# Regrouping the last weight tiles' rows of y: one late group of 16 rows for all batches and a third mid group moved on the SP queue

## The chip, the cores and the metric

The kernel runs on one NeuronCore of a Trainium2 chip. The metric is the device time of one execution in microseconds, as the median of five runs. The engines named below are PE (matmul; PEld is its weight load), DVE, ACT, POOL and SP. SP does no arithmetic here: it only issues DMAs. DMAs issued by SP, ACT and POOL each have a queue.

## What is computed

Attention with a forget gate on 8 batches, 8 heads, 576 positions and head size 64 gives x (8 x 576 x 512). Then x is mixed in the frequency domain: the first 64 modes of a real FFT over the positions are each multiplied by their own complex 512 x 512 matrix, and the inverse FFT gives y.

```
X = np.fft.rfft(x, axis=1)
Xr, Xi = (np.real(X[:, :n_modes]), np.imag(X[:, :n_modes]))
Yr = np.einsum('bmd,mde->bme', Xr, w_r) - np.einsum('bmd,mde->bme', Xi, w_i)
Yi = np.einsum('bmd,mde->bme', Xr, w_i) + np.einsum('bmd,mde->bme', Xi, w_r)
Y[:, :n_modes] = Yr + 1j * Yi
y = np.fft.irfft(Y, n=S, axis=1)
u = x + y
return (u + np.maximum(u @ w_ch, 0.0))
```

The inverse FFT is a matmul with a constant basis: per batch, 128 rows (64 modes, real and imaginary) by 576 positions. The kernel also needs u @ w_ch; it forms it as x @ w_ch plus the basis times (Y @ w_ch), so that each group of rows of Y is needed twice: as it is (called t=0) and times w_ch (t=1).

## The kernel before

**Weights.** `moe_w_r` and `moe_w_i` (together 134 MB in float32) are streamed through a ring of bfloat16 tiles, one tile after the other, by DMAs that POOL issues (`emit_w_load`, `pool_dma` at L90). There are NT = 64 tiles. The first 32 run beside the attention and cover the first two quarters of the input channels for all modes. The last 32 cover the second half of the channels, two modes each; a tile's index g (0 to 31) names its modes, and so the four rows of Y per batch that it completes. `tile_of` (L84) gives the order: g = 16 to 31 first (tiles 32 to 47), then g = 0 to 15 (tiles 48 to 63). Every one of these tiles ends with `add_y` (L146), which writes its completed rows of Y, transposed (channels on the partitions), into `YTe` for g of 16 and more, else into one half of `YT2`.

**Three kinds of rows.** The 64 rows per batch of g = 16 to 31 are "early": `emit_y` turns them into rows for the inverse FFT, and `emit_part` (L843) adds their share to x and to x @ w_ch while the remaining weights still stream. The other 64 rows per batch come in two halves of 32:

- g = 0 to 7 (tiles 48 to 55) are the "mid" rows. `emit_mid(q)` (L834) is called twice, after tiles 56 and 57, each time for four batches: `y_rows` does four transposes (L773, t=0) and four matmuls with w_ch (L777, t=1), and DVE and ACT copy each batch's 32 rows straight to their place in the tile `yy`.
- g = 8 to 15 (tiles 56 to 63) are the "late" rows, ready only when the last tile is done. Batches 0 to 3 go through `y_rows` at L995 right after that tile, batches 4 to 7 at L1032, in the output loop, after job 3.

A compute engine can copy batch 0's late rows directly to their place in `yy` (L996, L1000). The other batches' rows must change partitions: they are copied to a tile `yl` (L997, L1001; L1039, L1041) and then moved by small DMAs on POOL's queue (`emit_moves`, L904), 32 rows x 1 KB each: six for batches 1 to 3, and later eight for batches 4 to 7.

**The output loop.** There are 20 output jobs, five for each pair of batches: four of 256 positions of one batch, and as the fifth (jobs 4, 9, 14, 19) the last 64 positions of both batches. For each job PE sums two results in PSUM: pu (t=0, that is u) and pz (t=1, that is u @ w_ch). Each is the stored partial sum, passed through an identity, plus the basis times `yy`'s mid and late rows, 64 rows in one matmul. PE's matmuls of both kinds appear at L786. ACT copies pu to `uo` (L952, `emit_u`), DVE forms relu(pz) + u (L959, `emit_o`), and SP issues the output DMA (L971, or two DMAs of 64 rows at L966 for a fifth job; in job 19 alone the second of them is on ACT's queue). pu and pz of even and odd jobs have two PSUM places, so the sum pz of job n+2 can start only when DVE has read that of job n. The second late group borrows the unused halves of job 4's places. ACT's copy of job n+1 is written ahead of DVE's step of job n.

Of the kernel before, what the change touches and what calls it, by code (L numbers as in the profile page):

```python
# [9 lines left out]
BF16 = mybir.dt.bfloat16  # L10
# [11 lines left out]
def kernel(  # L22
# [11 lines left out]
    nc = tc.nc  # L34
    B, H, S, Dh = q.shape
    NM = moe_w_r.shape[0]
    D = H * Dh
# [5 lines left out]
    NDC = D // 128  # L43
# [22 lines left out]
    late = {}  # L66
# [17 lines left out]
    def tile_of(n):  # L84
        if n < NTH:
            return divmod(n, NG)
        return 2, (n - NTH + GL) % NTH

    def pool_dma(dst, src):
        tc.keep_in_program_order(nc.gpsimd.dma_start(dst, src))  # L90
# [36 lines left out]
    def emit_modes(n, fill=None):  # L127
# [17 lines left out]
            ]  # L145
        def add_y(mi0, mi1):  # L146
            n8 = (mi1 - mi0) * 2
            w = HM if g >= GL else HM // 2
            yt = late["YTe"] if g >= GL else late["YTs"][2 * g // GL]
            c0 = (g * nm + mi0) * 2 % w  # L150
            nc.vector.tensor_tensor(  # L151
                _strided(
                    yt[:, 0, 0, c0 : c0 + 1], [[B * w, NDC], [w, B], [1, n8]]
                ),
                _strided(A[:, 0, mi0, 0:1], [[nm * 2 * B, NDC], [1, B], [B, n8]]),
                _strided(
                    Yacc[:, 0, g * nm + mi0, 0:1],
                    [[NM * 2 * B, NDC], [1, B], [B, n8]],
                ),
                ALU.add,  # L160
            )
# [571 lines left out]
    with ExitStack() as bctx:  # L733
        bsb = bctx.enter_context(tc.tile_pool(name="bsb", bufs=1))
        YTe = bsb.tile([128, NDC, B, HM], BF16, name="YTe")
        YT2 = xtpool.tile([128, 2, NDC, B, HM // 2], BF16, tag="XT3", name="YT2")
        late["YTe"], late["YTs"] = YTe, [YT2[:, 0], YT2[:, 1]]
        HS = [slice(0, HM), slice(HM, 128)]
        BIe = [bsb.tile([128, SP], BF16, name=f"BIe{h}") for h in range(2)]
        BIl = bsb.tile([128, SP], BF16, name="BIl")  # L740
# [20 lines left out]

        yy = yls = xTs = None

        def row_slot(q, j, t, i):
            p0 = HM * ((j + t) % 2) + H2 * i
            return yy[p0 : p0 + H2, 1, 2 * q + j // 2, t, :]

        H2 = HM // 2

        def y_rows(yt, b0, ply, plw):  # L770
            cols = lambda eb: _strided(yt[:, eb, b0, 0:1], [[1, 128]])
            for eb in range(NDC):
                nc.tensor.transpose(  # L773
                    ply[:, eb * 128 : (eb + 1) * 128], cols(eb), ident_bf[:, :]
                )
            for eb in range(NDC):
                nc.tensor.matmul(  # L777
                    plw,
                    lhsT=cols(eb),
                    rhs=wch[:, eb, :],  # L780
                    start=(eb == 0),
                    stop=(eb == NDC - 1),
                )

        def add(p, lhsT, rhs, first):
            return nc.tensor.matmul(  # L786
# [7 lines left out]
        with ExitStack() as cctx:  # L794
# [39 lines left out]
            def emit_mid(q):  # L834
                pyw = psBig.tile([128, D], F32, tag="big", name="pyw")
                yp = psBig.tile([128, D], BF16, tag="big", name="yp")
                y_rows(YT2[:, 0], 4 * q, yp[:, :], pyw[:, :])
                for j in range(4):
                    rows = slice(H2 * j, H2 * j + H2)
                    nc.vector.tensor_copy(row_slot(q, j, 0, 0), yp[rows, :])  # L840
                    nc.scalar.copy(row_slot(q, j, 1, 0), pyw[rows, :])

            def emit_part(b, sb):  # L843
                pA = psBig.tile([128, D], F32, tag="big", name="pA")
# [19 lines left out]
            for bp in range(B // 2):  # L864
                parts += [(bp, None)]
                parts += [(b, sb) for b in (2 * bp, 2 * bp + 1) for sb in range(4)]
                parts += [(2 * bp, 4)]
            nx = done = 0
            while nmode < NT - 1:
                emit_modes(nmode)  # L870
                if nmode != late["nx"]:
                    next_w()
                nmode += 1
                if nmode == NTH + GL // 4:
                    open_late()
                if nmode > NTH + 6 and nmode % 4 and nx < B:
                    emit_xw(nx)
                    nx += 1
                if nmode > NT - GL:
                    assert nx == B  # L880
                    while done < (nmode - NT + GL) * (len(parts) - 2) // (GL - 2):
                        a, sb = parts[done]
                        emit_y(a) if sb is None else emit_part(a, sb)
                        done += 1
                if 0 <= nmode - NT + GL // 2 - 1 < 2:
                    emit_mid(nmode - NT + GL // 2 - 1)
            for a, sb in parts[done:]:
                emit_part(a, sb)

# [10 lines left out]
            for name in ("psE", "psU")  # L900
        )
        psPair = [{"u": psE, "z": psE}, {"u": psU}]

        def emit_moves(t, q, js):  # L904
            for j in js:
                pool_dma(
                    row_slot(q, j, t, 1), yls[q][H2 * j : H2 * j + H2, t, :]
                )

        def pieces(job):  # L910
            b, sb, nb = job
# [40 lines left out]
                nc.scalar.copy(uo[:, 0, bs, :], ps[0][:, bs, :])  # L952
            return uo

        def emit_o(job, ps, uo, split=False, last=False):
            b, sb, nb = job
            for i in range(2 if split else 1):
                bs = slice(i, i + 1) if split else slice(0, nb)
# [3 lines left out]
                )  # L962
                if sb == 4:
                    for h in range(2):
                        eng = nc.scalar if last and h else nc.sync
                        eng.dma_start(  # L966
                            out[b + h, 512:576, :],
                            uo[64 * h : 64 * h + 64, 1, 0, :],
                        )
                else:  # L970
                    nc.sync.dma_start(  # L971
                        out[b, 128 * sb : 128 * sb + 256, :].rearrange(
                            "(p r) e -> p r e", r=2
                        )[:, bs, :],
                        uo[:, 1, bs, :],
                    )
# [15 lines left out]
        ply = psL.tile([128, D], F32, tag="A", name="ply")  # L992
        ply = ply[:, 0 : D // 2].bitcast(BF16)
        plw = psL.tile([128, D], F32, tag="A", name="plw")
        y_rows(YT2[:, 1], 0, ply[:, :], plw[:, :])  # L995
        nc.vector.tensor_copy(row_slot(0, 0, 0, 1), ply[0:H2, :])  # L996
        nc.scalar.copy(yls[0][:, 0, :], ply[:, :])  # L997
        emit_moves(0, 0, (1,))
        run(terms(jobs[0], ps, 0, "y"))
        nc.vector.tensor_copy(row_slot(0, 0, 1, 1), plw[0:H2, :])  # L1000
        nc.vector.tensor_copy(yls[0][:, 1, :], plw[:, :])  # L1001
        emit_moves(1, 0, (1,))
        for j in (2, 3):
            for t in range(2):
                emit_moves(t, 0, (j,))
        lctx.close()
        psPair[1]["z"] = bctx.enter_context(
            tc.tile_pool(
# [4 lines left out]
        for n, job in enumerate(jobs):  # L1013
# [14 lines left out]
                run(zs)  # L1028
            else:
                run(zs, us)  # L1030
            if n == 3:
                y_rows(  # L1032
                    YT2[:, 1], 4, nxt[1][:, 1, 0 : D // 2].bitcast(BF16), nxt[0][:, 1, :]
                )
            if not last:
                uo_n = emit_u(jobs[n + 1], nxt)
            emit_o(job, ps, uo, n == 0, last)
            if n == 3:
                nc.scalar.copy(yls[1][:, 1, :], nxt[0][:, 1, :])  # L1039
            if n == 4:  # L1040
                nc.vector.tensor_copy(  # L1041
                    yls[1][:, 0, :], ps[1][:, 1, 0 : D // 2].bitcast(BF16)
                )
                for j in range(4):
                    for t in range(2):
                        emit_moves(t, 1, (j,))
            if not last:
                ps, uo = nxt, uo_n
# [28 lines left out]
```

## Time and profile before

| what | time |
|---|---|
| median of 5 runs | 439.18 us (437.88 to 442.24) |
| profiled execution | 438.02 us |
| its span | 436.0 us |
| PE busy | 362.5 us (83%) |
| DVE busy | 263.5 us (60%) |
| ACT busy | 224.9 us (52%) |
| mean granted PE clock | 0.846 |

All times of the trace are counted from the span's start. The profiled execution's own time includes 2.0 us around the span. Some points in time on the way to the end:

| event | us |
|---|---|
| last weight DMA issued by POOL | 384.48 |
| tile 60's matmuls start | 385.03 |
| tile 61's matmuls start | 388.63 |
| tile 62's matmuls (wait of 1.24 for their weights) | 394.18 |
| last tile's last eight matmuls start | 399.20 |
| first late group (L773) starts | 400.04 |
| first output DMA issued | 403.59 |
| second late group (L773) starts | 407.07 |
| its eight moves on POOL | 411.14 to 415.06 |
| last output DMA issued (ACT's queue) | 430.92 |

A busy engine in such a table need not be the limit: the share is an average over the attention, the weight stream and the output loop, and the change touches only the last 50 us. There the order in time, and which wait ends last, tell more than the shares.

### The profile page before, as it was taken

The numbers are of one execution on the slowest core, as the hardware profiler recorded it, in microseconds if no ns is written. First come the engines' busy times: TensorE is split into PE (matmuls) and PEld (weight loads), VectorE is DVE, ScalarE is ACT, GpSimd is POOL, SyncE is SP. The second block draws the span as 40 slices with busy tenths as digits, with TensorE's granted clock in tenths as the row PEclk, the third lists the DMA queues.
The fourth block names the chain that finished last, engine by engine and source line by source line (L and its number), as shares of the span: only waits on it lengthen the run. The fifth ranks groups of instructions, "written<-read, shape, count | busy, mean of one in ns | idle before, by whom it ended". The sixth has DMA issues, their size and how long they took to land.

```text
span 436.0 us, 12178 instructions
## 1 busy us (share of the span) xinstructions
PE 362.5 (83%) x5247; PEld 248.9 (57%) x5265; DVE 263.5 (60%) x658; ACT 224.9 (52%) x340; POOL 128.7 (30%) x202
## 2 busy tenths in 40 slices
PE   2687699999897977778878798799999978798983
PEld 1454566776665655565656666666665545454541
DVE  5687788877555655656556577623324545554774
ACT  3689377875636446355354644143344433543662
POOL 7333332153233232332332222232232223200400
PEclk9997699998856668668556869599999999989998
DMA  8999999999999999999999999999999999993797
GB/s 181 235 235 241 234 235 239 236 212 235 234 214 238 226 222 236 211 236 232 216 237 212 211 211 212 212 210 211 211 212 212 210 211 211 211 211 67 251 378 282
DMA packets 50181, 97.33 MB, mean 223 GB/s; under 512 B 3504, under 2 KB 12208, under 8 KB 50128
## 3 DMA queue, kind: packets, MB, share of 16 engines
q0 software_dynamic: 46688, 86.39, 101.1%
q1 hardware_dynamic: 3360, 10.05, 6.4%
q8 instruction: 41, 0.67, 0.6%
q10 hardware_dynamic: 80, 0.13, 0.1%
q14 instruction: 12, 0.10, 0.1%
HBM read 163.73 MB, written 9.44 MB: 397 GB/s over the span
## 4 chain that ended last, share of the span: by engine, by line
PE 35%; DMA 26%; ACT 12%; DVE 9%; issue 4%; SPq 0%; DVEq 0%; POOL 0%; ACTq 0%
DMA wb<-in_moe_w_i_dram 26%; ACT E L559 8%; PE pav L597 8%; PE ps L552 6%; PE A L186 6%; PE tp L500 5%; PE px L640 3%; PE pz L786 2%; PE vp L524 2%; ACT KT L513 2%; DVE QTs L515 2%; PE pu L786 2%; DVE XT L654 1%; DVE uo L959 1%; DVE E L574 1%
## 5 line engine op out<-in xcount | busy, mean ns | idle before, releaser
L559 ACT ACTIVATE E<-ps 128x1024 bf16<-128x1024 f32 (+1 forms) x128 | 101.3, 853 | 25.3 <-PE ps L552 16.0
L186 PE MATMUL A<-XT,wb 128*128 128x16 bf16 x1984 | 70.4, 181 | 13.5 <-DMA wb<-in_moe_w_i_dram 9.1
L90 POOL DMA_DIRECT2D wb<-in_moe_w_r_dram x64 | 42.5, 663 | 128.6 <-PE A L186 32.3
L186 PEld LDWEIGHTS <-wb 128*128 128x128 bf16 x1984 | 63.5, 99 | 28.0 <-issue 11.7
L552 PE MATMUL ps<-QTs,KT 64*128 64x64 bf16 (+4 forms) x384 | 58.0, 326 | 16.0 <-ACT E L559 14.7
L90 POOL DMA_DIRECT2D wb<-in_moe_w_i_dram x64 | 42.3, 661 | 78.2 <-DMA wb<-in_moe_w_i_dram 36.5
L597 PE MATMUL pav<-va,E 128*128 128x65 bf16 (+1 forms) x1088 | 55.2, 210 | 4.5 <-DVE x_all L619 3.6
L597 PEld LDWEIGHTS <-E 128*128 128x128 bf16 (+1 forms) x1088 | 45.6, 114 | 19.4 <-issue 9.0
L574 DVE TENSOR_TENSOR E<-E,trimask 128x256 bf16<-128x256 bf16 (+2 forms) x128 | 37.1, 301 | 20.3 <-ACT E L559 20.1
L517 ACT COPY VT<-tp 128x640 bf16<-128x640 bf16 (+1 forms) x32 | 23.2, 756 | 32.7 <-PE tp L500 32.6
L825 ACT CAST XW<-pxw 128x512 bf16<-128x512 f32 x36 | 20.7, 586 | 34.7 <-PE pxw L818 29.9
L861 ACT CAST XW<-pB 128x512 bf16<-128x512 f32 x36 | 21.0, 585 | 31.7 <-PE pB L786 25.0
L552 PEld LDWEIGHTS <-KT 64*128 64x128 bf16 x384 | 19.5, 99 | 30.6 <-issue 21.5
L860 DVE CAST x_all<-pA 128x512 bf16<-128x512 f32 x36 | 24.9, 691 | 15.3 <-PE pA L786 14.4
L818 PE MATMUL pxw<-wch,yy 128*128 128x512 bf16 x133 | 32.9, 379 | 1.1 <-issue 0.5
L513 ACT COPY KT<-tp 128x640 bf16<-128x640 bf16 (+1 forms) x32 | 22.1, 754 | 22.2 <-PE tp L500 22.2
L515 DVE COPY QTs<-tp 128x640 bf16<-128x640 bf16 (+1 forms) x32 | 23.2, 766 | 14.3 <-PE tp L500 14.2
L619 DVE TENSOR_TENSOR x_all<-pav,rcp 128x384 bf16<-128x384 f32 x64 | 29.1, 454 | 0.8
L608 DVE RECIPROCAL rcp<-pav 128x6 f32<-128x6 f32 x64 | 12.1, 189 | 22.7 <-PE pav L597 21.9
L959 DVE SCALAR_TENSOR_TENSOR uo<-pz,uo 128x1024 f32<-128x1024 f32 (+1 forms) x21 | 22.0, 1070 | 5.8 <-PE pz L786 3.5
L151 DVE TENSOR_TENSOR YTe<-A,Yacc 128x128 bf16<-128x128 f32 x16 | 5.9, 368 | 32.2 <-PE A L186 32.2
L786 PEld LDWEIGHTS <-ident_bf 64*64 64x64 bf16 (+1 forms) x300 | 15.4, 107 | 16.0 <-issue 7.4
(143 smaller groups left out, 634.6 us busy)
## 6 DMA issues: line engine op xcount, KB each, us to landing
wb<-in_moe_w_r_dram POOLq DMA_DIRECT2D x62, 512.0 KB, 16.6
wb<-in_moe_w_i_dram POOLq DMA_DIRECT2D x62, 512.0 KB, 17.5
out_dram<-uo SPq DMA_DIRECT2D x15, 512.0 KB, 3.9
stv<-in_v_dram POOLq DMA_DIRECT2D x10, 576.0 KB, 15.1
stk<-in_k_dram POOLq DMA_DIRECT2D x11, 288.0 KB, 15.2
stq<-in_q_dram POOLq DMA_DIRECT2D x11, 288.0 KB, 15.1
wx<-in_v_dram POOLq DMA_DIRECT2D x5, 576.0 KB, 15.1
wx<-in_k_dram POOLq DMA_DIRECT2D x5, 288.0 KB, 14.8
```

The lines of the kernel that those rows point to most:

```text
L90: tc.keep_in_program_order(nc.gpsimd.dma_start(dst, src))
L186: nc.tensor.matmul(A[:, eb, mi, :], lhsT=w_of(mi, eb * 128), rhs=x_of(m), start=(i == 0), stop=(i == len(terms) - 1),)
L513: nc.scalar.copy(rows(KTs[pr % 2][:, :, 0:S]), tv)
L515: nc.vector.tensor_copy(rows(QT[pr][:, :, :]), tv)
L552: nc.tensor.matmul(ps[:, b, o : o + n], lhsT=KTs[pr % 2][bs, h, jb * 128 : (jb + 1) * 128], rhs=QT[pr][bs, h, jb * 128 + c0 : jb * 128 + c ...
L559: nc.scalar.activation(E[:, :, piece * 512 : piece * 512 + w], ps[:, :, 0:w], ACT.Exp, scale=scale,)
L574: nc.vector.tensor_tensor(dg, dg, tr, ALU.mult)
L597: nc.tensor.matmul(pav[64 * half : 64 * half + w, slot, :], lhsT=E[:, b, c : c + (w - 1) * st + 1 : st], rhs=va[:, jb, b, :], start=(n == ...
L619: nc.vector.tensor_tensor(xo, pi, ri, ALU.mult)
L786: return nc.tensor.matmul(p, lhsT=lhsT, rhs=rhs, start=first, stop=not first, skip_group_check=True)
L818: nc.tensor.matmul(pxw[:, :], lhsT=xT[:, eb, i * 128 : (i + 1) * 128], rhs=wch[:, eb, :], start=(eb == 0), stop=(eb == NDC - 1),)
L959: nc.vector.scalar_tensor_tensor(uo[:, 1, bs, :], ps[1][:, bs, :], 0.0, uo[:, 0, bs, :], ALU.max, ALU.add,)
```

## The change

The order of the last 16 tiles becomes g = 0 to 7, 12 to 15, 8 to 11 (`g ^ 4`). The 32 late rows per batch are split into two groups of 16. Those of g = 12 to 15 (tiles 56 to 59) are a third mid group, in `YTn`: `emit_mid(2)`, after tile 60, takes all eight batches in one pass of `y_rows` (8 x 16 columns), copies the results whole into `yls[1]` with one DVE and one ACT instruction, and moves every batch's 16 rows to `yy` with sixteen DMAs on SP's queue. Those of g = 8 to 11 (tiles 60 to 63) stay late, in `YTl`: one `y_rows` after the last tile takes all eight batches, so the pass after job 3 is gone, with its copies and its eight moves. Batch 0's 16 rows are still copied directly; batches 1 to 7 take fourteen moves of 16 rows on POOL's queue, issued one after the other. In every fifth job, and not only in the last, the second output DMA of 64 rows goes on ACT's queue. The number of passes of `y_rows` for mid and late rows stays at four.

```diff
     def tile_of(n):
         if n < NTH:
             return divmod(n, NG)
-        return 2, (n - NTH + GL) % NTH
+        g = (n - NTH + GL) % NTH
+        return 2, g ^ 4 if GL // 2 <= g < GL else g
...
-            w = HM if g >= GL else HM // 2
-            yt = late["YTe"] if g >= GL else late["YTs"][2 * g // GL]
-            c0 = (g * nm + mi0) * 2 % w
+            yt, w, c0 = late["YT"](g)
+            c0 += mi0 * 2
...
+        def yt_of(g):
+            r = 2 * M2 * g
+            if g >= GL:
+                return YTe, HM, r % HM
+            if r < H2:
+                return YTm, H2, r
+            return (YTl if r < H2 + H4 else YTn), H4, r % H4
...
-        def row_slot(q, j, t, i):
-            p0 = HM * ((j + t) % 2) + H2 * i
-            return yy[p0 : p0 + H2, 1, 2 * q + j // 2, t, :]
+        def row_slot(b, t, r0, n):
+            p0 = HM * ((b + t) % 2) + r0
+            return yy[p0 : p0 + n, 1, b // 2, t, :]
...
+        def emit_moves(yl, r0, b, t, eng):
+            p0 = H4 * b
+            ins = eng.dma_start(row_slot(b, t, r0, H4), yl[p0 : p0 + H4, t, :])
+            if eng is nc.gpsimd:
+                tc.keep_in_program_order(ins)
...
-                y_rows(YT2[:, 0], 4 * q, yp[:, :], pyw[:, :])
+                y_rows((YTm, YTn)[q // 2], 4 * q % B, yp[:, :], pyw[:, :])
+                if q == 2:
+                    nc.vector.tensor_copy(yls[1][:, 0, :], yp[:, :])
+                    nc.scalar.copy(yls[1][:, 1, :], pyw[:, :])
+                    for b in range(B):
+                        for t in range(2):
+                            emit_moves(yls[1], H2 + H4, b, t, nc.sync)
+                    return
...
+            MID = (NT - GL // 2 + 1, NT - GL // 2 + 2, NT - GL // 4 + 1)
...
-                if 0 <= nmode - NT + GL // 2 - 1 < 2:
-                    emit_mid(nmode - NT + GL // 2 - 1)
+                if nmode in MID:
+                    emit_mid(MID.index(nmode))
...
-                        eng = nc.scalar if last and h else nc.sync
+                        eng = (nc.sync, nc.scalar)[h]
...
-        y_rows(YT2[:, 1], 0, ply[:, :], plw[:, :])
-        nc.vector.tensor_copy(row_slot(0, 0, 0, 1), ply[0:H2, :])
+        y_rows(YTl, 0, ply[:, :], plw[:, :])
+        nc.vector.tensor_copy(row_slot(0, 0, H2, H4), ply[0:H4, :])
         nc.scalar.copy(yls[0][:, 0, :], ply[:, :])
-        emit_moves(0, 0, (1,))
+        emit_moves(yls[0], H2, 1, 0, nc.gpsimd)
         run(terms(jobs[0], ps, 0, "y"))
-        nc.vector.tensor_copy(row_slot(0, 0, 1, 1), plw[0:H2, :])
+        nc.vector.tensor_copy(row_slot(0, 1, H2, H4), plw[0:H4, :])
         nc.vector.tensor_copy(yls[0][:, 1, :], plw[:, :])
-        emit_moves(1, 0, (1,))
-        for j in (2, 3):
+        emit_moves(yls[0], H2, 1, 1, nc.gpsimd)
+        for b in range(2, B):
             for t in range(2):
-                emit_moves(t, 0, (j,))
+                emit_moves(yls[0], H2, b, t, nc.gpsimd)
...
-            if n == 3:
-                y_rows(
-                    YT2[:, 1], 4, nxt[1][:, 1, 0 : D // 2].bitcast(BF16), nxt[0][:, 1, :]
-                )
...
-            if n == 3:
-                nc.scalar.copy(yls[1][:, 1, :], nxt[0][:, 1, :])
-            if n == 4:
-                nc.vector.tensor_copy(
-                    yls[1][:, 0, :], ps[1][:, 1, 0 : D // 2].bitcast(BF16)
-                )
-                for j in range(4):
-                    for t in range(2):
-                        emit_moves(t, 1, (j,))
```

## The prediction

> **What bounds the kernel now.** I read the chain of waits in order of time first: it says which work cannot move. Its columns are start, length, what.
>
> ```profile
> 356.00 18.25 DMA wb<-in_moe_w_i_dram
> 374.25 0.29 issue
> 374.54 19.60 DMA wb<-in_moe_w_i_dram
> 394.14 0.05 issue
> 394.18 0.91 PE A L186 x30
> ...
> 399.20 0.36 PE A L170 x8
> ...
> 407.07 0.38 PE pz L773 x4
> 407.46 0.05 issue
> 407.51 0.81 PE pu L777 x3
> ...
> 410.44 0.41 DVE yl L1041
> ```
>
> Up to 399.2 the weight stream sets the pace; from there to the end it is a PE/DVE loop, in which the second late group's transposes and matmuls (L773, L777 at 407) and the copy of their result (L1041) stand on the path. Next, busy time by stretch: the stretch, its length, busy us of PE, PEld, DVE, ACT and POOL, granted clock, DMA share, GB/s.
>
> ```profile
> 385.00:390.00 5.00, 4.66 (x89) 3.07 (x88) 3.05 (x5) 2.34 (x4) 0.01 (x1) 1.00 1.12 212
> 394.00:399.30 5.30, 5.08 (x90) 2.86 (x91) 1.88 (x4) 1.17 (x2) 0.00 (x0) 1.00 0.46 87
> 402.00:404.00 2.00, 1.92 (x24) 0.91 (x21) 1.84 (x4) 1.88 (x3) 1.49 (x3) 1.00 0.07 16
> 404.00:431.00 27.00, 23.10 (x263) 12.39 (x260) 21.18 (x21) 16.54 (x19) 5.40 (x12) 1.00 0.91 327
> ```
>
> The DMA engines are full until about 390 (1.12: transfers overlap in an engine). In the last 5 us of weights the share is 0.46, yet PE still waits for them: about half of the engines have finished, and the others carry the end. Then DVE in order of time, for the rhythm of the output jobs (job 3 is the second of 405.80, job 6 starts at 412.70; job 8 starts at 415.53, job 11 at 419.46):
>
> ```profile
> 405.80 2.58 DVE L959 SCALAR_TENSOR_TENSOR uo<-pz,uo 128x1024 f32<-128x1024 f32 x2 [0.51 <-ACT uo L952]
> 412.70 2.43 DVE L959 SCALAR_TENSOR_TENSOR uo<-pz,uo 128x1024 f32<-128x1024 f32 x2 [0.64 <-PE pz L786]
> 415.53 1.82 DVE L959 SCALAR_TENSOR_TENSOR uo<-pz,uo 128x1024 f32<-128x1024 f32 x2 [0.40 <-PE pz L786]
> 419.46 2.43 DVE L959 SCALAR_TENSOR_TENSOR uo<-pz,uo 128x1024 f32<-128x1024 f32 x2 [0.29 <-PE pz L786]
> ```
>
> **Removed from the tail: the second late group.** Its PE work is 1.27 us (407.05 to 408.32), straight on the chain. Its DVE copy L1041 (0.41 us) holds the PSUM tile that job 6 wants: PE idles 0.31 us for it at 410.90. Together about 1.7 us. What would be late next? DVE is busy with job 3 until 405.80+2.58=408.38 whatever PE does, so the gain is measured from there. From the end of job 3 to the start of job 6 takes 412.70-408.38=4.32 us. The same piece of the next five jobs, without a late group, is from the end of job 8 (415.53+1.23=416.76) to 419.46: 2.70 us; one round later it is again 2.70 (423.53 to 426.23). So the tail gains **1.62 us**, after which the rhythm of 6.76 us per five jobs goes on as before. The eight POOL moves at 411 to 415 go too; nothing waited for them.
>
> **Added under the weights: the third mid group**, between the tiles at 385.03 and 388.63. Its PE cost is that of the first mid group at 367.90: 1.1 us. Of this 0.55 hides in the wait before 389.18, and the rest in the 1.24 us wait for weights at 394.18. DVE pays 0.41 and ACT 0.59, on engines that have 2.66 and 2.14 us of work in the 5 us from 389. If that cover were gone it would cost its 1.1 us. I take **0**.
>
> **Sixteen moves on SP, 16 KB each.** The t=0 rows are copied at about 389.5, the t=1 rows at 390.4. SP has no other work until the first output at 403.59. These are the prices of an issue (minimum/median/maximum in ns), and of a move on POOL:
>
> ```profile
> L971 SPq DMA_DIRECT2D out_dram<-uo x17: 332/333/550, 403.6 to 430.3; - x17
> L966 SPq DMA_DIRECT2D out_dram<-uo x7: 472/895/1707, 410.5 to 430.9; - x7
> L90 POOL DMA_DIRECT2D yy<-yl x14: 496/496/522, 402.1 to 414.6; - x14
> ```
>
> At 0.5 us (the small L966 at its least, 0.47; the two loads at the start took 0.58 and 0.56) the last is issued at 390.4+15x0.5=398, well ahead of 403.6. At 0.33 it is 395.4; at 1.18, the second L966 of a pair at 418.33, it is 408: that is a rival below.
>
> Here a rule decides. The Trainium skill, DMA: Bandwidth & Descriptors, section Issuing engines are not separate DMA queues, says that transfers from any issuing engine share the same 16 DMA engines and that another issuer saves only issue time. By the row alone (SP empty, share 0.46) the moves would be free; by the rule they take engine time from the weights, and the engines that still carry weights set 399.2. The price comes from 402 to 404, where nearly nothing else runs: 16 GB/s x 2 us is one 32 KB move, at 0.07 x 2 = 0.14 us of all 16 engines. Half the bytes cost half, 0.07, and sixteen of them **1.1 us** on each engine; with the overlap of 1.12 I take 1.0. PE had waits of only 0.41 and 0.51 us for its last weights (398.25, 399.20) and sits on them, so what delays them delays everything. The ends: 0, if the moves use only what finished engines or waiting ones leave; 2.5 us, if each holds an engine as long as a weight packet (a 512 KB load takes 2.5 us of the stream and is 256 packets, 16 for each engine, so 0.155 us each, times 16). I take 1.0, since the small move is the nearer row. Without the moves the sum would be -1.4, with them -0.4.
>
> Will batch 0's moves be there for its matmuls at 401.2? A weight load takes 16 to 17 us from issue to landing, and behind that queue a move of 390.4 would land at 407. The same page, section Queues, rings and completion order, says that an engine goes round its queues packet by packet. By that the move lands in the 2 to 4 us of the POOL moves (1.7/2.5/3.9, part of them beside outputs), near 394. I take the rule: no stall. The trace of before has no move beside weights, so it can't confirm this.
>
> **The remaining late group and its POOL moves.** One pass of transposes and matmuls after the last tile, as now, with 16 rows instead of 32 in the two direct copies: a copy's time goes with its columns (0.41 for 32 and for 128 partitions), so 0. Fourteen POOL moves at 0.5 us run from 402.1 to about 409.5. Batch 1's two are first, as now; batch 4's leave by 407 and are wanted near 415. Nobody waits: 0. All PE reads of late rows now wait for an SP landing as well as a POOL one; these waits are on PE's queue and bounded at 0 to 0.3.
>
> **One small output in two on ACT's queue**, in three more jobs. ACT pays 0.56 us (its issue at 430.92) after DVE finishes job 9 (417.35), so until 417.96; its next copy started at 417.94 anyway, having waited 0.59 for PE: 0. If the issue takes 1.18 that copy ends 0.6 late, 0.2 past the start of job 11. Three times: 0 to 0.6. SP is relieved by as much, but nobody on the loop waits for SP: at 422.30 a DVE wait of 0.40 is put down to an output DMA, yet the same job 6.77 us earlier and later waits the same 0.40 for PE. For the last two parts together I take **0.2**.
>
> **Sum**: -1.62 + 0 + 1.0 + 0.2 = **-0.4 us**. The profiled execution took 438.02 us (span 436.0 and 2.0 around it), so 437.6; the median of the runs is 439.18, 1.16 above that execution, and the difference carries over: **438.8 us**. A measurement of this kernel can't tell less than 0.5%, 2.2 us, from no change.
>
> **Rivals.**
> - *The moves are free* (-1.62 + 0 + 0.2 = -1.4, **437.8 us**; with nothing paid on ACT 437.6). For it: from 394 the share is 0.46. Against: the engines that PE waits for are just the full ones.
> - *The moves stall the last weights* (slower). Place: the landings that PE waits for at 398.25 and 399.20. Price: up to 0.155 us for each of 16 moves, 2.5 us. It decides from (1.62-0.2)/16 = 0.09 us per move on. Sum -1.62+2.5+0.6 = +1.5: **440.7 us**. For it: both streams write SBUF through the same engines at share 1.12. Against: the measured 0.07.
> - *SP becomes the bound*: 16 issues at 1.18 us end near 409, and the first output leaves 5.5 us late. The outputs fill 0.91 x 27 + 0.61 x 5 = 27.6 us of all engines (0.61 after 431), less 1.0 for halved POOL moves; from 409.9 that ends at 436.5, where the last now lands at 434.7: +1.8, **441.0 us**. Against: only L966 under full output load shows such issues.
> - That the change doesn't do what it says: POOL's eight late moves must vanish by the new order of tiles, and do; I give it nothing.
>
> **Chances.** Forecast 0.40, free moves 0.28, stalled weights 0.20, SP 0.12. The likeliest's own range is 438.0 to 439.7. For eight in ten I go from 436.8 (free moves, with 0.8 for a scatter of medians and no more) to 441.3 (the two slow cases at their prices). Faster by over 0.5% (below 437.0) needs free moves and a low draw: 0.15. Slower by over 0.5% (above 441.4) takes the upper half of both slow cases and their joining: 0.18. Within: 0.67.
>
> **What would show it.** Right: job 3's end to job 6's start near 2.7 us; no L773 or L777 in the tail but one; the last weights landing about 1 us later against the tile before the third mid group; SP's moves at 0.5 us, done by 399. Free moves: the last wait for weights unmoved. SP: moves still issuing at 403.6. ACT: DVE waiting for L952 after each small output. I am wrong if PE waits for SP's landings at 401, or if the rhythm of 6.76 us changes.

## The result, and the profile after

| | before | after |
|---|---|---|
| median of the runs (lowest to highest), us | 438.57 (436.83 to 442.24, 79 runs) | 437.57 (435.81 to 440.76, 44 runs) |
| profiled execution, us | 438.02 | 436.93 |
| its span, us | 436.0 | 435.2 |

The ratio of the times is 0.997, with a 95% interval of 0.9961 to 0.998. That is 1.3 us less (0.9 to 1.7): within the 0.5% that was called no change, but, with this many runs, clear of zero. In "before" all runs of the kernel before that stood beside a run of another kernel are counted, so its median differs from the five runs of the prediction. Every ratio below is taken against the runs of the kernel before on the same chip.

The chain of waits of the kernel after, in order of time (start, length, what):

```profile
374.07 19.78 DMA wb<-in_moe_w_i_dram
...
393.89 0.91 PE A L186 x30
394.80 0.57 PE pA L806
395.37 0.43 PE pB L806
...
408.45 1.24 DVE uo L981
```

The weight stream still sets the pace up to 393.89. After it the picture differs from before: no DMA stands between there and the end of the weights, and single matmuls of the parts take 0.43 to 0.57 us. The late group (L787 and L791 at 401.4 to 402.6) now stands on the chain once. The output jobs on DVE (start, length of the group, idle time before it in brackets):

```profile
407.10 3.20 DVE L981 SCALAR_TENSOR_TENSOR uo<-pz,uo 128x1024 f32<-128x1024 f32 x3 [0.51 <-ACT uo L974]
...
415.22 1.82 DVE L981 SCALAR_TENSOR_TENSOR uo<-pz,uo 128x1024 f32<-128x1024 f32 x2 [0.34 <-PE pz L806]
```

Job 3 starts at 408.45, job 8 at 415.22: 6.77 us. Before, they started at 407.15 (its end at 408.38 less its own 1.23) and 415.53: 8.38 us. The tail is **1.61 us** shorter, and its first five jobs now have the rhythm that the others had (6.76). But job 3 itself starts 1.30 us later than before, although the last weight load was issued 0.4 us earlier. So something ahead of the tail costs time, and the two sums differ by little. By stretch (length, busy us of PE, PEld, DVE, ACT, POOL, granted clock, DMA share, GB/s):

```profile
394.00:399.30 5.30, 5.03 (x67) 2.67 (x69) 1.88 (x4) 1.17 (x2) 0.00 (x0) 0.68 0.60 119
404.00:431.00 27.00, 23.25 (x266) 12.95 (x264) 21.95 (x22) 17.40 (x20) 6.20 (x13) 1.00 0.90 333
```

In the last 5 us of weights the DMA engines moved 119 GB/s instead of 87; without the moves, in a run below whose last load goes out 0.9 us later, it is 100. And the granted clock is 0.68, where it was 1.00. No part of the sum had this.

The moves and the outputs by their issues (ns, minimum/median/maximum, first and last start in us), and below the moves the time to their landing:

```profile
L801 SPq DMA_DIRECT2D yy<-yl x16: 582/588/1477, 388.4 to 398.0; - x16
L801 POOL DMA_DIRECT2D yy<-yl x14: 484/484/509, 403.4 to 410.1; - x14
...
DMA to landing us min/median/max: 1.6/3.9/4.8
```

```profile
L988 SPq DMA_DIRECT2D out_dram<-uo x4: 472/514/575, 410.3 to 430.6; - x4
L988 ACTq DMA_DIRECT2D out_dram<-uo x4: 504/507/569, 410.3 to 430.6; - x4
```

SP's sixteen issues are over at 399.4, ahead of its first output at 404.9. No move took more than 4.8 us, against 14.7 us and more for a load, so none lay behind the weights' queue. The last weight load of each kernel, its issue and its landing, before first:

```profile
L90 POOL DMA_DIRECT2D wb<-in_moe_w_i_dram x1: 528/528/528, 384.5 to 384.5; - x1
...
DMA to landing us min/median/max: 14.7/14.7/14.7
```

```profile
L91 POOL DMA_DIRECT2D wb<-in_moe_w_i_dram x1: 528/528/528, 384.1 to 384.1; - x1
...
DMA to landing us min/median/max: 15.4/15.4/15.4
```

It takes **0.7 us** longer. Over the last five loads of that weight the delay grows from 0.2 to 0.7 us, while the moves are issued.

One more difference is at the very end. From the last issue of an output to the end of the span is 436.0-430.92 = 5.1 us before and 435.2-430.6 = 4.6 us after, in which the last outputs landed, counted from their issue, before and after in

```profile
DMA to landing us min/median/max: 3.5/3.7/3.9
DMA to landing us min/median/max: 2.9/3.1/3.2
```

### The profile page after: what moved, and what is told of

The parts are those of the page before. It is cut to its first block, busy times and chain, and to the rows that moved or that the text cites. A ratio compares the mean times of both kernels' runs of the same rounds, so it can differ in the third digit from the quotient of the medians.

```text
span 435.2 us, 12214 instructions
## 1 busy us (share of the span) xinstructions
PE 360.8 (83%) x5247; PEld 247.3 (57%) x5265; DVE 263.2 (60%) x658; ACT 225.2 (52%) x340; POOL 128.8 (30%) x202
## 4 chain that ended last, share of the span: by engine, by line
PE 35%; DMA 26%; ACT 12%; DVE 10%; issue 5%; DVEq 0%; POOL 0%; ACTq 0%
DMA wb<-in_moe_w_i_dram 26%; ACT E L559 8%; PE pav L597 7%; PE ps L552 6%; PE A L186 6%; PE tp L500 5%; PE pz L806 3%; PE px L640 3%; DVE QTs L515 2%; ACT KT L513 2%; PE vp L524 2%; DVE uo L981 2%; PE pu L806 2%; DVE XT L654 1%; DVE E L574 1%
## 5 line engine op out<-in xcount | busy, mean ns | idle before, releaser
L559 ACT ACTIVATE E<-ps 128x1024 bf16<-128x1024 f32 (+1 forms) x128 | 101.5, 855 | 24.0 <-PE ps L552 14.7
L552 PE MATMUL ps<-QTs,KT 64*128 64x64 bf16 (+4 forms) x384 | 56.0, 315 | 18.3 <-ACT E L559 17.0
L597 PE MATMUL pav<-va,E 128*128 128x65 bf16 (+1 forms) x1088 | 53.6, 206 | 4.1 <-DVE x_all L619 3.5
L597 PEld LDWEIGHTS <-E 128*128 128x128 bf16 (+1 forms) x1088 | 44.1, 112 | 19.9 <-issue 9.6
```

The costliest lines, as they stand in the source:

```text
L552: nc.tensor.matmul(ps[:, b, o : o + n], lhsT=KTs[pr % 2][bs, h, jb * 128 : (jb + 1) * 128], rhs=QT[pr][bs, h, jb * 128 + c0 : jb * 128 + c ...
L559: nc.scalar.activation(E[:, :, piece * 512 : piece * 512 + w], ps[:, :, 0:w], ACT.Exp, scale=scale,)
L597: nc.tensor.matmul(pav[64 * half : 64 * half + w, slot, :], lhsT=E[:, b, c : c + (w - 1) * st + 1 : st], rhs=va[:, jb, b, :], start=(n == ...
```

## The experiments

Since profiles of different executions start their last load at different times, they are compared from that issue on. **Front** is the time from it to the start of PE's last eight weight matmuls (L170 in both kernels), and **tail** the time from there to the end of the span. Front, tail and clock are those of one profiled execution of each kernel; ratio and median are of its timed runs. The experiments' numbers stand in this table; the text takes the experiments in the order in which they were made.

| kernel | ratio, 95% | median, us | front | tail | half clock after tile 62 |
|---|---|---|---|---|---|
| before | 1 | 438.57 | 14.72 | 36.80 | no |
| after | 0.997 (0.9961 to 0.998) | 437.57 | 16.44 | 34.70 | yes |
| after, outputs not split | 0.9977 (0.9961 to 0.9993) | 437.66 | 16.00 | 35.01 | yes |
| before, outputs split | 1.0006 (0.9988 to 1.0025) | 438.57 | 14.71 | 36.85 | no |
| after without SP moves | 0.9956 (0.9939 to 0.9973) | 436.90 | 16.21 | 34.46 | yes |
| after, moves on POOL | 0.9994 (0.9978 to 1.001) | 438.08 | 16.27 | 34.52 | yes |
| before with 84 moves | 1.010 (1.0061 to 1.0139) | 443.32 | – | – | yes, at 400.8 |
| after again | 0.9979 (0.9964 to 0.9993) | 437.16 | 15.99 | 34.64 | yes |
| after, PE filled | 0.9977 (0.9961 to 0.9994) | 436.37 | 15.28 | 34.67 | no |
| before, PE filled | 0.9999 (0.9977 to 1.002) | 438.37 | 14.71 | 36.44 | no |
| without moves, filled | 0.9976 (0.996 to 0.9993) | 436.49 | 14.72 | 34.47 | no |
| after with eight old moves | 1.0023 (1.0008 to 1.0038) | 439.39 | 16.42 | 36.74 | yes |
| moves spread, filled | 0.9956 (0.994 to 0.9973) | 436.65 | 15.03 | 34.98 | no |

Theory at the start: the tail's 1.6 us and a shorter drain of the outputs are the gain, the delay of the last weights by the moves is the price. Rivals: the moves are free and something else is late; the output split makes the shorter drain.

### The output split: undone, and alone

```diff
-                        eng = (nc.sync, nc.scalar)[h]
+                        eng = nc.scalar if last and h else nc.sync
...
```

This is the kernel after with the split undone (in the last job it stays, as before). The second kernel is before with the same two lines exchanged the other way.

> The kernel after, but the second 64-row output of jobs 4, 9 and 14 is issued by SP again, as before. Theory: the split over two queues keeps the output of jobs 5, 10, 15 from being issued late (in the trace of before SP issued job 10's at 419.60, 0.4 us after DVE had it; after, at once) and so shortens the last landings by about 0.6 us; then this kernel loses about 0.5 us against the kernel after: ratio to before 0.998, and the last outputs land 3.5 us or more after their issue, with SP issues of 1.2 us in the small pairs. Rival: the shorter end has another cause (half the moves); then the ratio stays at 0.997 and the last outputs land about 3.0 us after their issue.

> The kernel before with the split of the small outputs over SP and ACT alone. Theory: -0.5 us, ratio 0.9988, last outputs landing in 3.0 us instead of 3.6 to 3.8. Rival, as in the prediction: SP's relief is worth nothing and ACT pays 0 to 0.6 us: ratio 1.000 to 1.0014.

Neither time moved clear of its interval: 0.9977 without the split in the kernel after, 1.0006 with it in the kernel before. The landing of the last outputs tells which part owns the shorter drain; without the split in the kernel after it is

```profile
DMA to landing us min/median/max: 2.8/3.1/3.3
```

and with the split in the kernel before

```profile
DMA to landing us min/median/max: 3.6/3.8/3.9
```

So the split doesn't bring the earlier landings; something else that the change does must. A smaller gain isn't excluded: without the split the tail is 35.01, 0.3 us longer than in the kernel after. The price of ACT's issue (504 to 569 ns) is nowhere seen in DVE's waits, which agree within 0.04 us with and without the split.

### Without the moves, and with them on POOL's queue

```diff
-                    for b in range(B):
-                        for t in range(2):
-                            emit_moves(yls[1], H2 + H4, b, t, nc.sync)
...
+                if nmode == NT - 10:
+                    nc.vector.memset(yy[:, 1, :, :, :], 0.0)
```

The first kernel leaves the third mid group's rows out of the result (zeros stand in their place); all else is done. The second issues the same moves on POOL:

```diff
-                            emit_moves(yls[1], H2 + H4, b, t, nc.sync)
+                            emit_moves(yls[1], H2 + H4, b, t, nc.gpsimd)
```

> The kernel after without the sixteen moves on SP (the rows of the third mid group are left out, zeros stand in their place from a memset ahead of tile 54). Theory: the moves are what delays the last weights; without them the last weight DMA lands 14.7 us after its issue, as before (15.4 after), and the time falls by about 0.7 us against the kernel after: ratio to before 0.9954. Rival: the landing stays at 15.4 and the ratio at 0.997, the delay being that of one execution.

> The kernel after with the sixteen moves issued on POOL's queue behind the weights. Theory: on the weights' own queue each engine takes them after its weights; the last weight DMA lands 14.7 us after its issue again, the moves land together at 399 to 401, just ahead of job 0's matmuls, and the time is 0.7 us under the kernel after: ratio 0.9954. Rival: batch 0's moves come too late and PE stands still at about 402 for 1 us or more: ratio 0.998 or above. Third: they delay the weights just as from SP: ratio 0.997.

Without moves the last weight load lands in 14.7 us again, as before the change:

```profile
L91 POOL DMA_DIRECT2D wb<-in_moe_w_i_dram x1: 531/531/531, 384.9 to 384.9; - x1
...
DMA to landing us min/median/max: 14.7/14.7/14.7
```

So the moves alone cause the 0.7 us. The ratio, 0.9956, is the one expected, but its interval reaches to 0.9973, so it isn't told apart from the 0.997 of the kernel after. And the front did not go back: 16.21 against 14.72 before. The reason is in the clock of the same kernel's last stretch of weights:

```profile
394.00:399.30 5.30, 4.67 (x62) 2.48 (x62) 1.37 (x3) 0.81 (x2) 0.00 (x0) 0.68 0.53 100
```

0.68, as in the kernel after. The half clock thus doesn't need the moves, and it was a cost that the theory had to take in.

On POOL the moves did not behave as SP's. In order of time on POOL's queue:

```profile
389.54 1.06 POOL L801 DMA_DIRECT2D yy<-yl  x2 [4.40 <-DMA wb<-in_moe_w_i_dram]
392.09 0.49 POOL L801 DMA_DIRECT2D yy<-yl  x1 [1.49 <-DMA wb<-in_moe_w_r_dram]
...
399.56 4.79 POOL L801 DMA_DIRECT2D yy<-yl  x10 [0.73 <-DMA wb<-in_moe_w_i_dram]
404.71 6.22 POOL L801 DMA_DIRECT2D yy<-yl  x13 [0.36 <-DVE yl L1023]
```

Up to 399.56 the issues wait until a weight load has landed, some move takes up to 10.0 us to land, and ten of them are issued in a row only from then on. The reason stands in the trace's instructions: POOL's DMAs take eight semaphores in turn (99 to 106), and each of these moves waits for its own, so for the landing of the DMA that was issued eight before it. It is thus a limit of this program, and not one that the run shows of POOL's queue. The late moves start behind them, at 404.71, which is 0.8 us later after the last load's issue than in the kernel after. The last weights are spared (14.7 us), yet the kernel is no faster than before, 0.9994. Its profiled execution took 437.08 us, its median is 438.08, and the profile doesn't show where the runs lose that microsecond; this expectation failed, and why is open. What can be read is that on POOL, in this program, the moves wait for the loads, and that on SP they don't.

### Eighty-four moves in the kernel before

To price a move with a signal well above the scatter, `emit_part` of the kernel before got small moves of 16 rows x 1 KB on SP, 84 in all, each to a tile that is not used until the tail.

```diff
+                for src in (xs[0:16], zs[0:16], zs[16:32]):
+                    if late["dose"] < 84:
+                        j = late["dose"] % 16
+                        late["dose"] += 1
+                        nc.sync.dma_start(
+                            yls[1][16 * (j // 2) : 16 * (j // 2) + 16, j % 2, :], src
+                        )
...
```

> The kernel before with 84 extra moves of 16 rows x 1 KB on SP under the weights of tiles 49 to 60, copying finished rows to a tile that is not yet used; nothing waits for them but one another. Theory: each move takes 0.044 us from the weight stream (0.7 us for 16, from the last landing of before and after): 84 x 0.044 = +3.7 us, ratio 1.0084. The prediction's price of 0.0625 gives +5.3 us, ratio 1.012. Rival: the engines that the weights leave idle carry them: 0, ratio 1.000.

4.4 us longer (2.7 to 6.1), which is 0.052 us for each move (0.032 to 0.073). The load of the chain of waits that PE waits for at tile 62 is, here,

```profile
378.04 21.39 DMA wb<-in_moe_w_i_dram
```

and ends at 399.43; before, it ended at 394.14. Of the 5.29 us between them 0.56 were there already before the first move (the same chain's load at 294.44 instead of 293.88). So 4.7 us for 84 moves, **0.056 us each**, while the engines were full:

```profile
376.00:382.00 6.00, 5.95 (x77) 3.32 (x74) 4.94 (x10) 5.24 (x10) 1.82 (x3) 1.00 1.15 218
```

The rival of free moves falls. Sixteen of them at 0.056 are 0.9 us; in the kernel after 0.7 was measured, which fits engines that are full for the first of the sixteen only (a share of 0.60 from 394 on).

### The half clock: after once more, and PE kept busy

What do the kernels with the half clock share? PE's matmuls after tile 62 in the kernel after, one by one:

```profile
393.89 0.91 PE L186 MATMUL A<-XT,wb 128*128 128x16 bf16 x30 [1.37 <-DMA wb<-in_moe_w_i_dram]
394.73 0.64 PE L806 MATMUL pA<-x_all,ident_bf 128*64 128x512 bf16 x1
...
398.25 0.56 PE L170 MATMUL A<-XT,wb 128*128 128x16 bf16 x16
```

These parts (the matmuls of `emit_part`) run from 394.73 to 398.25, 3.5 us; before the change the same parts ran from 395.02 to 396.87, 1.85 us. Windows of 3.41 us around it, first after:

```profile
391.29:394.70 3.41, 2.04 (x44) 1.26 (x38) 1.38 (x2) 1.17 (x2) 0.00 (x0) 1.00 0.95 183
394.70:398.11 3.41, 3.41 (x21) 1.25 (x17) 1.06 (x2) 0.59 (x1) 0.00 (x0) 0.51 0.66 130
```

then before:

```profile
377.10:380.50 3.40, 1.35 (x36) 1.07 (x36) 0.79 (x2) 0.58 (x1) 1.10 (x2) 1.00 1.12 211
380.50:383.90 3.40, 3.18 (x15) 1.17 (x14) 1.07 (x3) 0.61 (x2) 0.53 (x1) 0.50 1.13 211
...
390.80:394.20 3.40, 2.16 (x23) 0.93 (x20) 2.08 (x3) 1.76 (x3) 0.00 (x0) 1.00 0.95 178
```

In both, half clock lasts one such window and follows one in which PE was busy for little of the time: 2.04 of 3.41 us (60%) after, 1.35 of 3.40 (40%) before. Before, it came at 380.5, where PE waits for weights anyway; its window at 390.8, 64% busy, was not followed by one. The Trainium skill, TensorE: Matmul & The Clock Gate, section Part 1, describes windows of 3.4 us, with the clock at half after an idle one and at full after a busy one; the lengths here agree. Its section HAM oscillation names idle gaps longer than that window as what to avoid. By that rule the kernel after is safe, since its longest wait there is 1.37 us; by the rows it pays. The rows decide: waits that add up to 40% of a window were enough here. They are no sure sign, though. In the filled kernel, which comes next, a window with PE busy for only 50% was followed by full clock, and in the kernel before with the split alone one with 59% (363.20 to 366.61) was too:

```profile
360.93:364.34 3.41, 1.70 (x16) 0.73 (x10) 1.02 (x2) 1.17 (x2) 0.71 (x1) 1.00 1.12 211
364.34:367.75 3.41, 3.24 (x52) 2.09 (x54) 1.71 (x3) 0.97 (x2) 1.01 (x2) 1.00 1.12 211
```

If the wait ahead of tile 62 is the cause, five matmuls that nobody reads, put in it, must take the half clock away. They were put into after, into before, and into the kernel without the moves, with after itself once more beside them.

```diff
+                if nmode == NT - 2:
+                    pf = psBig.tile([128, D], F32, tag="big", name="pf")
+                    for i in range(5):
+                        tc.keep_in_program_order(
+                            nc.tensor.matmul(
+                                pf[:, :], lhsT=ident_bf[:, :], rhs=wch[:, i % NDC, :],
+                                start=True, stop=True,
+                            )
+                        )
                 emit_modes(nmode)
```

> The kernel after once more, for a second profiled execution and a time on the same chip as the next three. Theory: the half clock of PE from 394.7 to 398.2 is no accident of one execution: with the third mid group the wait for tile 62's weights leaves PE busy 60 to 64% of a 3.4 us clock window, and the next window is granted half the clock (in the four profiles taken so far of kernels with the third mid group it was there each time). It shows again, ratio 0.997. Rival: the phase of the windows decides from execution to execution, and there is no half clock between 390 and 402 this time.

> The kernel after with five matmuls more (128x512, read by nobody) that fill the wait for tile 62's weights. Theory: no half clock after tile 62, the parts after it take 1.85 us instead of 3.5, and the time falls by the part of it that the weights do not hide, about 1.0 us: ratio to before 0.9946. Rival: in most timed executions there is no half clock there; then 0.997, or 0.9975 with the fill in the way.

> The kernel before with the same five matmuls. Theory: its profile shows full clock after tile 62, so nothing to gain: 0.999 to 1.001. Rival: the half clock falls there in many executions of before too, and the fill gains as much as in the kernel after: 0.9975.

> The kernel after without the sixteen moves on SP (third mid rows left out, zeros in their place) and with the five filling matmuls. Theory: with the clock out of the way what the moves cost shows: the last weights land 14.7 us after their issue and not 15.4, and the time is 0.7 us under the filled kernel with its moves: ratio 0.993. Rival: the late landing is hidden by PE's own work, and both filled kernels take the same time.

Filled, the kernel after has full clock in the window after the low one, and waits for its last weights again, as before the change:

```profile
394.70:398.10 3.40, 3.11 (x66) 1.96 (x63) 1.83 (x4) 1.17 (x2) 0.00 (x0) 1.00 0.66 132
```

```profile
399.93 0.36 PE L170 MATMUL A<-XT,wb 128*128 128x16 bf16 x8 [0.38 <-DMA wb<-in_moe_w_i_dram]
```

That separates two costs which hid each other. With full clock the front is 14.72 without the moves (as before the change) and 15.28 with them: **0.56 us** for the moves on PE. With the half clock the front of the kernel after and of its repeat is 16.44 and 15.99, another **0.7 to 1.2 us**, and the delay of the weights is hidden under it. Six unfilled kernels with the third mid group were profiled and all six have the half clock at this place; the three filled ones don't. So the half clock hangs on PE's wait for tile 62's weights.

That the third mid group brings it is less certain, since the old order has this wait too. It is 1.24 us long in the kernel before and 1.25 with the split alone, and 1.25 without the moves and with the moves on POOL, of which only the last two were given half clock. With the split alone the wait fell on the border of two windows (PE busy for 2.69 and 2.88 of 3.41 us); in the kernel before it lay in one window. In the kernel with 84 moves, in the old order, it was 1.59 us long, and half clock followed:

```profile
397.41:400.82 3.41, 1.82 (x42) 1.24 (x40) 1.06 (x2) 0.68 (x2) 0.00 (x0) 1.00 0.79 149
400.83:404.24 3.41, 3.41 (x34) 1.42 (x33) 1.44 (x3) 1.17 (x2) 0.00 (x0) 0.50 0.38 70
```

Where the windows lie against the work also differs between executions. Counted from the issue of the last load in steps of 3.41 us, they start 0.43 to 1.29 us after it in the six, but 2.88 in the kernel before and 2.36 with the split alone. These profiles don't exclude that this position, and not the new order, makes the difference.

The times don't show this gain: the 0.9946 and 0.993 that were expected of the filled kernels with and without moves both failed. By ratio the filled kernel (0.9977) and the repeat of after (0.9979) are the same, by median 0.8 us apart, and the intervals are some 0.7 us to each side. Filled with moves and filled without are not told apart either (0.9977 and 0.9976), and in the kernel before the filling changed nothing (0.9999), as expected. So the profiles show the two costs in the executions that they record; how many of the timed executions have the half clock is open.

### The drain: eight old moves put back

What else could shorten the drain? The change made fourteen late moves of 32 rows (448 KB) into fourteen of 16 rows (224 KB). Before, eight of them went at 411 to 415, for the second late group. Eight such moves (256 KB) were put back into the kernel after, on POOL after job 4, into a tile that nobody reads any more:

```diff
+            if n == 4:
+                for j in range(4):
+                    for t in range(2):
+                        rows = slice(32 * j, 32 * j + 32)
+                        pool_dma(yls[1][rows, t, :], yls[0][rows, t, :])
```

> The kernel after with eight moves of 32 rows more on POOL at job 4, as the kernel before has them there, copying rows to a tile that is free by then; nobody waits for them. Theory: what shortens the end in the kernel after (last outputs landing 2.8 to 3.1 us after their issue instead of 3.5 to 3.8) is the DMA work of those moves, about 1 us of all engines in a stretch where outputs fill them. With it back the last outputs land in 3.4 us or more, and the stretch from DVE's last step to the end is 0.5 us longer than in the kernel after. Rival: it is the order or the split of the outputs; then the landings stay at 2.8 to 3.1 us.

1.0023: slower than before the change, and 2.3 us above after. The output jobs on DVE keep their times (job 8 to the last one as in after, both 0.97 us later, as is the last load's issue), but the last outputs now land in

```profile
DMA to landing us min/median/max: 4.5/5.0/5.4
```

and the tail is 36.74 instead of 34.70. The stretch ahead of the end, first with the eight moves, then in the kernel after:

```profile
424.00:431.00 7.00, 5.51 (x64) 2.95 (x63) 5.73 (x7) 4.34 (x5) 0.00 (x0) 1.00 0.99 369
```

```profile
424.00:431.00 7.00, 4.76 (x56) 2.41 (x48) 5.50 (x5) 3.52 (x4) 0.00 (x0) 1.00 0.95 354
```

The DMA engines are busy for 0.99 of it, while DVE is done as early as in the kernel after. And 36.74 is nearly the tail that the kernel before had (36.80): with about as many bytes to move as before (480 KB to 448), the whole gain of the tail is gone, although the second late group stays away. So in these profiles the end follows how much the DMA engines have to carry. From 404 to the end they are busy for 0.90x27 + 0.51x4.2 = 26.4 us in the kernel after (0.51 is the share from 431 on), and for 27.6 us before by the prediction's own sum; the 224 KB that are gone are 1.0 of that 1.2 at the prediction's price (7 x 0.14). In this reading two things changed the drain: the output jobs end 1.61 us sooner, which alone would lengthen it by as much, and the moves' absence shortens it by 2.0, which leaves 0.4 of the 0.5 that was seen. What the run shows by itself is the 2.0. That is four times the 0.5 that was expected, and nearly twice the price of the eight moves (8 x 0.14 = 1.1); why, isn't shown.

The times agree with it: this kernel takes 1.0 us more than before (0.4 to 1.7), and if its tail is the old one in the timed runs too, that is what the front costs in them.

### Moves spread out, with PE filled

From these results a version was made that leaves the last weights less to wait for: of the sixteen moves only the four of batches 0 and 1 go under the weights, those of batches 2 and 3 go on POOL among the late moves, and those of batches 4 to 7 go on SP behind a two-element DMA that reads the first half of the last tile's result, so that they start after the weights; SP's moves keep the order of the program. PE is filled as above.

```diff
...
-                    for b in range(B):
+                    for b in range(2):
...
+            if mi == 1 and hf == 0:
+                tc.keep_in_program_order(
+                    nc.sync.dma_start(late["mark"][0:16, 0:2], YTl[0:16, 0, 0, 12:14])
+                )
+                for b in range(4, B):
+                    for t in range(2):
+                        emit_moves(yls[1], H2 + H4, b, t, nc.sync)
...
                 emit_moves(yls[0], H2, b, t, nc.gpsimd)
+                if b < 4:
+                    emit_moves(yls[1], H2 + H4, b, t, nc.gpsimd)
```

> The filled kernel with only batches 0 and 1 of the third mid group moved under the weights (4 moves on SP); batches 2 and 3 go on POOL's queue among the late moves, batches 4 to 7 on SP behind a small DMA that waits for the first half of the last tile. Theory: the last weights land 14.9 us after their issue instead of 15.2 to 15.4, so the front gains 0.4 us against the filled kernel; the tail carries twelve small moves more, of which eight fall before the outputs, and loses up to 0.2: about 0.2 to 0.4 us under the filled kernel, ratio 0.9955 if the fill is worth its 0.8 us and 0.997 if not. Rival: the moves on SP delay the first outputs and batch 4's rows, and it is no faster than the kernel after: 0.998.

0.9956, 1.9 us below before (1.2 to 2.6). The last weights land in 14.9 us and the front is 15.03, by 0.25 better than filled alone. What moves out of the front comes back in the drain: the last outputs land 3.7 to 4.2 us after their issue, and the tail is 34.98. It beats before; from after (0.997) it isn't separated.

## Why the prediction was right, and where its sum was not

Forecast: 438.8, 0.4 us less than before; measured 437.57, and by the ratio 1.3 us less. The direction was right, the time lies inside the range (436.8 to 441.3), and the likeliest case's mechanism, moves that delay the weights, was seen. But 437.57 lies below that case's own range (438.0 to 439.7) and is nearest to the case of free moves. Of the 1.2 us between forecast and measurement, 0.6 is the reference: 439.18 from five runs against 438.57 from 79. Point by point:

- **The second late group, -1.62.** Measured -1.61. Taking job 3's end as the fixed point, and the next round without a late group as the measure, gave the gain to 0.01 us. The rhythm of 6.76 us per five jobs is unchanged.
- **The third mid group, 0.** By itself it cost nothing: with PE filled and no moves the front is the old 14.72. But in all six unfilled profiles half clock follows the wait for tile 62, and it costs 0.7 to 1.2 us in them. This is a term that the sum lacks; whether the new order brings it or the position of the windows stays open. The view of granted clock by stretch would have raised the question: it shows a half clock in the kernel before at 380.5, hidden under a wait.
- **Sixteen moves, +1.0.** The mechanism was right and the size was not: 0.0625 us each were assumed, 0.056 were measured under full engines, 0.044 (0.7/16) at the place itself, and PE felt 0.56 us, where the clock lets it feel anything. The rule that another issuer saves only issue time decided rightly against the share of 0.46, which made the moves look free.
- **No stall for batch 0, issues at 0.5 us.** SP's issues took 0.588 us; the last began at 398.0, as forecast, because the first began at 388.4 instead of 389.5, and ended at 399.4 ("done by 399"). The landings took at most 4.8 us beside full weights instead of 2 to 4, and PE waited for none. The weights' own 15 us did not apply, as the packet-by-packet rule said.
- **The split and the extra waits, +0.2.** Neither was seen, but the timed intervals, some 0.7 us to each side, could hide it.
- **The removed POOL moves, 0.** This is the step of the sum that failed: "The eight POOL moves at 411 to 415 go too; nothing waited for them." No compute engine did, but the outputs share the DMA engines with them. The text of the rival on SP even has their price ("less 1.0 for halved POOL moves"), and left it out of the sum. Measured: 0.5 us less drain beyond the -1.61; and with such moves back in the tail, 2.0 of the 2.1 us of the two together are lost. In that profile even the -1.61 therefore hung on this step: that the change also halves the bytes to move was luck for a sum that gave it nothing.

In the profiles, with full clock, the terms add up to -1.61 - 0.5 + 0.56 = -1.55. With the half clock the front costs 1.3 to 1.7 instead of 0.56, which gives -0.4 to -0.8. The measured -1.3 (0.9 to 1.7) is nearer to the first; from the kernel with the eight moves the front of the timed runs is put at 1.0 (0.4 to 1.7), between the two. So the forecast of -0.4 was short by about 0.9 because it counted no gain in the drain (0.5), 0.4 too much for the moves and 0.2 for waits that weren't seen, less a part of the half clock. How large that part is in timed runs stays open.

The rivals: stalled weights and SP as the bound are excluded by the landings and issues above. Free moves, at 437.8 against 439.18, gave -1.4 and so nearly the measured size, for the wrong reason: the moves do delay the weights, and a gain that nobody had counted pays for it.

## What to carry to other kernels

A DMA that no instruction waits for still has a price where the outputs behind it fill the engines: count the bytes that a change adds to or takes from the stretch that drains last, even those with no reader on the critical path. When work is taken out of or moved within a stretch where PE waits for DMA, look at how busy PE stays over some microseconds as well as at the waits, since the clock of the stretch behind it can depend on that. And measure a gain in the tail from the last thing that the change leaves alone, here the end of job 3: that number came out exact, while everything ahead of it had moved by a microsecond.

## What was not expected of the hardware

- Half clock for 3.4 us followed windows of that length in which matmuls covered 60% of the time, with no single wait above 1.37 us; the kernel before, at 64%, was spared. In two other kernels (without moves, moves on POOL) windows of 63 and 64% were followed by half clock, and in two more windows of 50 and 59% were not, so the busy share alone doesn't settle it.
- A move of 16 x 1 KB on SP landed in at most 4.8 us (5.9 in the kernel with 84 of them) beside a weight stream whose loads took 15 to 20 us, and delayed that stream by 0.044 to 0.056 us.
- Eight moves of 32 KB, issued 15 to 20 us ahead of the last output, made the last outputs land 1.9 us later (5.0 against 3.1).
